# A fused attention, expert and MLP kernel: its float64 weight tiles decoded in another order, their remainders on VectorE

## The chip, the cores and the metric

The kernel runs on one core of a Trainium2 chip. The time is the device time of one execution in microseconds (us), the median of several. The five engines are TensorE (PE, with its weight loads shown apart as PEld), VectorE (DVE), ScalarE (ACT), GpSimd (POOL) and SyncE (SP, which here only issues DMAs). Each engine takes its instructions strictly in the order in which they stand in its own queue; an instruction that waits holds up all that stand behind it on that engine.

## The reference, cut to what matters

Three parts follow one another. A linear attention over (2, 8, 768, 48) gives 1536 token rows of 384. A mixture of 8 experts (width 1024) treats each row with the expert that its gate picks. A gated MLP of width 1536 ends it; its gate weights are drawn 200 times larger than usual.

```python
def _moe2_ref(x, w_gate, w_val, w_out) -> np.ndarray:
    gate = 1.0 / (1.0 + np.exp(-(x @ w_gate)))
    val = x @ w_val
    return (gate * val @ w_out).astype(np.float32)
```

The weights of the MLP arrive as float64. The kernel reads each as two 32-bit words and makes a float32 of it.

## The kernel before, in words

**Precision.** Every float32 product is made of three fp32r matmuls: an operand a is split into a high part (ACT casts it to fp32r) and a low part, the remainder (a less its high part, rounded to fp32r); high by high, high by low and low by high are summed in PSUM.

**The expert stage** (97.7 to 244 us of the trace) runs a loop over 64 steps, eight slices f of eight experts e. Step i holds `s1` (nine matmuls of 256 columns into `ph`, then `hh` on ACT at L825 and its remainder `hl` on DVE at L826), `s2` of three steps before, at two places of each expert the transposes and the split of the next expert's tokens (`etr`: `xh` or `xeh` on ACT at L807, `xl` or `xel` on DVE at L808), and `bg`, which splits one weight tile of 128x768: `rh` on ACT at L137, `rl` at L139, in odd steps on POOL and in even ones on DVE.

**The MLP stage** (from 244 us) takes the 1536 tokens in four blocks j of 384 and the width in twelve slices f. `mf(j,f)` is 18 matmuls of 384 columns into two PSUM tiles `pg`, nine for the gate and nine for the value. `gate` follows: sigmoid `sg` on ACT (L934), product `gg` on DVE (L936), its fp32r cast `gh` on ACT (L939) and its remainder `gl` on DVE (L940). `mo(j,f)` is nine matmuls that add the slice to the output in `po`. The two `pg` tiles have one buffer each: the next `mf` may write its gate half only once `sg` has read the one before, and its value half only once `gg` has. (The first `mf` of blocks 0 and 1 borrows tiles of `po` and waits for neither.) Two lanes run through the loop at L967: lane 0 does block 0 and then 2, lane 1, two steps later, block 1 and then 3. So the order on PE is `mf(0,0)`, `mf(0,1)`, `mo(0,0)`, `mf(0,2)`, `mo(0,1)`, `mf(1,0)`, and from there on one `mf` and one `mo` in turn, 27 matmuls to a gate, lanes alternating.

**The decoding.** A tile of 128x768 float64 weights is fetched by SP into `r64` (two buffers) and decoded in seven steps that `decode` (L151) returns as closures: o1 the magnitude from the upper word into `wf`, on ACT (L157); o2 a clamp (L160), o3 a shift (L163), o4 the sign (L167) and o5 the three bits from the lower word (L171), all on DVE; o6 the fp32r cast of the tile on ACT (L177) and its remainder, the tile less its cast, on POOL (L178); o7 the fetch of the tile two places later in `ORDER` (L149). `wf` has two buffers as well. Tiles 0 to 11 feed `mf`, tiles 12 to 17 feed `mo`. The first seven (`EARLY`) of `ORDER` are decoded in the expert stage, one closure a step from step 6 on (L900), into buffers named `ws`. The other eleven are decoded in the MLP loop, one tile to each k: o1 to o3 ahead of the gate of lane 0, o4 and o5 ahead of that of lane 1, o6 and o7 behind it; they go into the buffers `rh`, `rl` and `raw` (named `wr`) that the expert stage has left.

Nothing reorders any of this: the order of the calls is the order of each queue.

Of the kernel before, what the change touches and what calls it, by code (L numbers as in the profile page):

```python
# [7 lines left out]
F32 = mybir.dt.float32  # L8
# [25 lines left out]
WARM = 16  # L34
BG = (0, 0, 0, 0, 0, 0, 4, 3)
DP = 2
ORDER = (0, 1, 2, 12, 3, 4, 13, 5, 6, 14, 7, 8, 15, 9, 10, 16, 11, 17)
EARLY = 7
HPB = 6
OVP = 60  # L40
# [62 lines left out]
def body(tc, A, out):  # L103
    nc = tc.nc
    E = mybir.EngineType
    with ExitStack() as top, tc.manual_schedule():
# [37 lines left out]
        r64, wyh, wyl = {}, {}, {}  # L144
        spl, homes = [None], []

        def dfetch(n):
            r64[n] = spl[0].tile([128, 768, 2], I32, tag="r64", name="r64", bufs=2)
            nc.sync.dma_start(out=r64[n].rearrange("p a b -> p (a b)"), in_=wy[n])  # L149

        def decode(n):  # L151
            t = {}

            def o1():
                t["a"] = spl[0].tile([128, 768], F32, tag="wf", name="wf", bufs=2)
                t["i"] = t["a"].bitcast(I32)
                nc.scalar.activation(out=t["a"], in_=r64[n][:, :, 1].bitcast(F32), func=AF.Abs, scale=2.0 ** 16)  # L157

            def o2():
                nc.vector.tensor_scalar(out=t["a"], in0=t["a"], scalar1=2.0, scalar2=DMAX, op0=ALU.max, op1=ALU.min)  # L160

            def o3():
                nc.vector.tensor_scalar(out=t["i"], in0=t["i"], scalar1=4, scalar2=1, op0=ALU.logical_shift_left,  # L163
                                        op1=ALU.logical_shift_right)

            def o4():
                nc.vector.scalar_tensor_tensor(out=t["i"], in0=r64[n][:, :, 1], scalar=-2 ** 31, in1=t["i"],  # L167
                                               op0=ALU.bitwise_and, op1=ALU.bitwise_or)

            def o5():  # L170
                nc.vector.scalar_tensor_tensor(out=t["i"], in0=r64[n][:, :, 0], scalar=29, in1=t["i"],  # L171
                                               op0=ALU.logical_shift_right, op1=ALU.bitwise_or)
                r64.pop(n)

            def o6():
                wyh[n], wyl[n] = homes.pop(0)
                nc.scalar.copy(out=wyh[n], in_=t["a"])  # L177
                nc.gpsimd.tensor_sub(wyl[n], t["a"], wyh[n].bitcast(F32))  # L178

            def o7():  # L180
                k = ORDER.index(n)
                if k + 2 < 18:
                    dfetch(ORDER[k + 2])

            return [o1, o2, o3, o4, o5, o6, o7]

        scx, sci = [], []

# [505 lines left out]
        with ExitStack() as ctx:  # L694
# [98 lines left out]
            def eload(e, eng=nc.sync):  # L793
                xr[e] = mp.tile([128, 2, 384], F32, tag="xr", name="xr")
                after(eng.dma_start(out=xr[e], in_=xs_d[e * 1536:e * 1536 + 256, :].rearrange("(b p) d -> p b d", p=128)), scx)
# [52 lines left out]
                nc.vector.tensor_sub(XL[m][:, d], ys[e][m], XH[m][:, d].bitcast(F32))  # L848

            xt[0] = (xeh, xel)  # L850
            dops = [op for n in ORDER[:EARLY] for op in decode(n)]
            dops.reverse()
            fetch(sum(BG) + FIRST)
            eload(1)
            dfetch(ORDER[0])
            dfetch(ORDER[1])
            seq = [(e, f) for e in range(8) for f in range(8)]
# [47 lines left out]
        with ExitStack() as ctx:  # L905
# [9 lines left out]
            def mf(j, f):  # L915
                wh, wl = wyh[f], wyl[f]
                if f == 0 and j < 2 or f == 11 and j == 3:
                    pg = [pop.tile([128, 384], F32, tag="po0" if f else "po1", name="pg") for _ in range(2)]
                else:
                    pg = [pgp.tile([128, 384], F32, tag=f"pg{g}", name="pg") for g in range(2)]  # L920
                seq = [(g, kt) for g in range(2) for kt in range(3)]
                if j == f == 0:
                    seq = [(g, kt) for kt in (0, 2, 1) for g in range(2)]
                c = slice(j * 384, j * 384 + 384)
                last = 1 if j == f == 0 else 2
                for g, kt in seq:
                    w = slice((g * 3 + kt) * 128, (g * 3 + kt) * 128 + 128)
                    for n, (a, b) in enumerate(((wh, XH), (wl, XH), (wh, XL))):
                        nc.tensor.matmul(pg[g], a[:, w], b[kt][:, c], start=(kt == n == 0), stop=(kt == last and n == 2))  # L929
                return pg  # L930

            def gate(j, f, pg):
                sg = qp.tile([128, 384], F32, tag="sg", name="sg")
                nc.scalar.activation(out=sg, in_=pg[0], func=AF.Sigmoid)  # L934
                gg = qp.tile([128, 384], F32, tag="gg", name="gg")
                nc.vector.tensor_mul(gg, sg, pg[1])  # L936
                gh = qp.tile([128, 384], F32R, tag="gh", name="gh", bufs=7)
                gl = qp.tile([128, 384], F32R, tag="gl", name="gl", bufs=7)
                nc.scalar.copy(out=gh, in_=gg)  # L939
                nc.vector.tensor_sub(gl, gg, gh.bitcast(F32))  # L940
                gs[(j, f)] = (gh, gl)
# [21 lines left out]
            def lane(first, k):  # L963
                return (first + 2 * (k // 12), k % 12)

            todo = list(ORDER[EARLY:])
            for k in range(24 + SKEW):  # L967
                ops = decode(todo.pop(0)) if todo else []
                for op in ops[:3]:
                    op()  # L970
                if k < 24:
                    gate(*lane(0, k), mf(*lane(0, k)))
                if 0 < k <= 24:
                    mo(*lane(0, k - 1))
                for op in ops[3:5]:
                    op()
                b = k - SKEW
                if b >= 0:
                    gate(*lane(1, b), mf(*lane(1, b)))
                if 0 < b <= 23:  # L980
                    mo(*lane(1, b - 1), (0, 1, 2) if b < 20 else (0, 1) if b < 22 else (0,))
                for op in ops[5:]:
                    op()
            for f, t in ((7, 2), (8, 2), (9, 2), (9, 1), (11, 0), (10, 1), (11, 1), (10, 2), (11, 2)):
                mo(3, f, (t,))

# [16 lines left out]
```

## Time and profile before

| | us |
|---|---|
| median of 3 runs | 483.82 (483.56 to 485.02) |
| the profiled execution, its own time | 483.43 |
| its span, first to last instruction | 481.7 |
| PE busy in the span | 445.0 (92%) |
| DVE busy | 291.4 (60%) |
| ACT busy | 223.0 (46%) |
| POOL busy | 178.9 (37%) |

The profiled execution's own time is 1.7 us more than its span. PE is busy nearly throughout, so that what matters is where it is not, and who it waits for there; an engine with a low share of busy time can still be the one that is waited for.

### The profile page before, as it was taken

Reading aid. Unit: us, or ns where it says so; the run is one execution under the profiler, and the core shown is the slowest. Engines: PE = TensorE matmul, PEld = TensorE weight load, DVE = VectorE, ACT = ScalarE, POOL = GpSimd, SP = SyncE. Lnnn points to the kernel's source line nnn. Section 1 sums busy time; section 2 is a strip of 40 time slices with the busy share of each in tenths; the row PEclk is TensorE's granted clock in tenths of the full one; section 3 lists DMA queues with packets and bytes.
Section 4 is the critical chain, followed back from the end, with each engine's and each line's share of the span. In section 5 each row is a group of like instructions: output and inputs, shape, how many; then the busy total and the mean of one; then the engine's idle time right before and its main releaser. Section 6 shows DMA issues by size and latency. Waiting matters only on the chain.

```text
span 481.7 us, 8681 instructions
## 1 busy us (share of the span) xinstructions
PE 445.0 (92%) x3354; PEld 429.0 (89%) x3356; DVE 291.4 (60%) x506; ACT 223.0 (46%) x481; POOL 178.9 (37%) x126
## 2 busy tenths in 40 slices
PE   6979987599998999899989899999999999999995
PEld 2668986599988999898988799999999999999995
DVE  4897997678999899987347676566322222212221
ACT  2676877546845775675333433433232322222231
POOL 4786938635866555565002221121120200000022
PEclk9979999799999999999999999999999999999999
DMA  7999942779899777862003322320010100000011
GB/s 212 350 336 309 283 186 84 250 294 208 226 210 353 257 243 243 259 231 71 3 9 123 116 83 67 126 71 0 1 49 1 49 1 0 1 1 1 1 49 49
DMA packets 23708, 65.11 MB, mean 135 GB/s; under 512 B 4592, under 2 KB 8816, under 8 KB 23664
## 3 DMA queue, kind: packets, MB, share of 16 engines
q1 hardware_dynamic: 21600, 59.80, 40.1%
q0 software_dynamic: 1920, 4.73, 2.6%
q8 instruction: 27, 0.44, 0.4%
q14 instruction: 17, 0.14, 0.1%
q10 hardware_dynamic: 144, 0.00, 0.0%
HBM read 56.65 MB, written 7.87 MB: 134 GB/s over the span
## 4 chain that ended last, share of the span: by engine, by line
PE 44%; DVE 3%; issue 3%; ACT 1%; POOL 1%; POOLq 0%; ACTq 0%; DVEq 0%
PE pg L929 28%; PE po L953 5%; PE po L952 5%; PE po L951 4%; DVE wf L160 1%; PE ph L822 1%; DVE gg L936 1%; POOL out_dram L190 1%; DVE wf L167 1%; ACT wf L157 1%; PE py L841 1%; PE py L843 0%; PE py L842 0%; DVE wf L171 0%; DVE gl L940 0%
## 5 line engine op out<-in xcount | busy, mean ns | idle before, releaser
L936 DVE TENSOR_TENSOR gg<-sg,pg 128x384 f32<-128x384 f32 x48 | 26.6, 553 | 93.7 <-PE pg L929 91.7
L929 PE MATMUL pg<-xhi,ws 128*128 128x384 f32 x240 | 61.6, 337 | 4.7 <-ACT sg L934 3.0
L939 ACT CAST gh<-gg 128x384 fp32r<-128x384 f32 x48 | 24.7, 514 | 83.9 <-DVE gg L936 83.9
L139 POOL TENSOR_TENSOR rl<-raw,rh 128x768 fp32r<-128x768 f32 x25 | 49.3, 1975 | 26.6 <-ACT rh L137 24.9
L190 POOL DMA_INDIRECT out_dram<-ob,ids x12 | 11.7, 975 | 123.8 <-ACT ob L960 121.4
L934 ACT ACTIVATE sg<-pg 128x384 f32<-128x384 f32 x48 | 23.5, 490 | 70.6 <-PE pg L929 70.6
L137 ACT CAST rh<-raw 128x768 fp32r<-128x768 f32 x64 | 53.2, 839 | 4.3 <-PE py L842 4.2
L841 PE MATMUL py<-hh,rh 128*128 128x256 f32 x192 | 54.2, 282 | 0.0
L842 PE MATMUL py<-hl,rh 128*128 128x256 f32 x192 | 53.1, 276 | 0.0
L843 PE MATMUL py<-hh,rl 128*128 128x256 f32 x192 | 53.1, 276 | 0.0
L929 PE MATMUL pg<-xlo,rh 128*128 128x384 f32 x144 | 48.7, 338 | 0.0
L929 PE MATMUL pg<-xhi,rh 128*128 128x384 f32 x144 | 48.6, 338 | 0.0
L929 PE MATMUL pg<-xhi,rl 128*128 128x384 f32 x144 | 48.6, 337 | 0.0
L929 PEld LDWEIGHTS pg<-xhi,ws 128*128 128x128 f32 x240 | 43.1, 188 | 6.2 <-ACT sg L934 3.6
L139 DVE TENSOR_TENSOR rl<-raw,rh 128x768 fp32r<-128x768 f32 x32 | 42.3, 1321 | 6.1 <-ACT rh L137 5.6
L940 DVE TENSOR_TENSOR gl<-gg,gh 128x384 fp32r<-128x384 f32 x48 | 26.8, 558 | 27.8 <-ACT gh L939 27.8
L178 POOL TENSOR_TENSOR rl<-wf,rh 128x768 fp32r<-128x768 f32 x8 | 14.7, 1837 | 70.5 <-ACT rh L177 70.5
L929 PE MATMUL pg<-xlo,ws 128*128 128x384 f32 x120 | 40.2, 335 | 0.0
L841 PEld LDWEIGHTS py<-hh,rh 128*128 128x128 f32 x192 | 36.1, 188 | 0.1
L825 ACT ACTIVATE hh<-ph 128x256 fp32r<-128x256 f32 x64 | 24.8, 388 | 24.6 <-PE ph L822 23.6
L842 PEld LDWEIGHTS py<-hl,rh 128*128 128x128 f32 x192 | 36.1, 188 | 0.0
L843 PEld LDWEIGHTS py<-hh,rl 128*128 128x128 f32 x192 | 36.0, 188 | 0.0
(187 smaller groups left out, 1230.7 us busy)
## 6 DMA issues: line engine op xcount, KB each, us to landing
raw<-in_wx_dram SPq DMA_DIRECT2D x64, 384.0 KB, 5.4
r<-in_wy_dram SPq DMA_DIRECT2D x18, 768.0 KB, 4.4
dm<-in_dm_dram SPq DMA_DIRECT2D x8, 672.0 KB, 11.6
kr<-in_kr_dram SPq DMA_DIRECT2D x8, 576.0 KB, 11.7
v<-in_v_dram SPq DMA_DIRECT2D x8, 384.0 KB, 10.7
xs_d<-zero SPq DMA_DIRECT2D x8, 384.0 KB, 10.6
xr<-xs_d SPq DMA_DIRECT2D x8, 384.0 KB, 4.3
cat<-in_cax_dram SPq DMA_DIRECT2D x1, 404.0 KB, 13.6
```

The lines of the kernel that those rows point to most:

```text
L137: nc.scalar.copy(out=h, in_=t)
L139: (nc.gpsimd if pool else nc.vector).tensor_sub(rl[n % NR], t, h.bitcast(F32))
L825: nc.scalar.activation(out=hh, in_=ph, func=AF.Relu)
L841: nc.tensor.matmul(y, wh[:, w], hh, start=(f == 0 and m != 1), stop=False, skip_group_check=True)
L842: nc.tensor.matmul(y, wh[:, w], hl, start=False, stop=False, skip_group_check=True)
L843: nc.tensor.matmul(y, wl[:, w], hh, start=False, stop=(f == 7), skip_group_check=True)
L929: nc.tensor.matmul(pg[g], a[:, w], b[kt][:, c], start=(kt == n == 0), stop=(kt == last and n == 2))
L936: nc.vector.tensor_mul(gg, sg, pg[1])
L939: nc.scalar.copy(out=gh, in_=gg)
L940: nc.vector.tensor_sub(gl, gg, gh.bitcast(F32))
L952: nc.tensor.matmul(po[j][t], gh[:, a], wl[:, w], start=False, stop=False)
L953: nc.tensor.matmul(po[j][t], gl[:, a], wh[:, w], start=False, stop=(f == 11))
```

## The change

`decode` hands back eight closures in place of seven: the remainder becomes o8 and goes from POOL to DVE. `ORDER` is changed so that a tile for `mo` comes one place earlier.

In the expert stage the seven early tiles keep one closure a step, but the fetch (o7) comes ahead of the cast (o6), and the last of the seven steps now does the cast and the remainder together.

In the MLP stage the eleven tiles are taken in pairs (n, m), three groups of closures to a pair: o1 of n, the two remainders (o8) of the pair before, o2 and o3 of n; then o4, o5, fetch and cast of n, o1 and o2 of m; then o3, o4, o5, fetch and cast of m. One group stands behind each gate, of lane 0 and of lane 1 alike, beginning behind the first gate; before, a tile's steps began ahead of the gate of lane 0.

```diff
-ORDER = (0, 1, 2, 12, 3, 4, 13, 5, 6, 14, 7, 8, 15, 9, 10, 16, 11, 17)
+ORDER = (0, 1, 2, 12, 3, 4, 13, 5, 14, 6, 7, 15, 8, 9, 16, 10, 11, 17)
...
                 nc.scalar.copy(out=wyh[n], in_=t["a"])
-                nc.gpsimd.tensor_sub(wyl[n], t["a"], wyh[n].bitcast(F32))
+
+            def o8():
+                nc.vector.tensor_sub(wyl[n], t["a"], wyh[n].bitcast(F32))
...
-            return [o1, o2, o3, o4, o5, o6, o7]
+            return [o1, o2, o3, o4, o5, o6, o7, o8]
...
-            dops = [op for n in ORDER[:EARLY] for op in decode(n)]
+            dops = []
+            for n in ORDER[:EARLY]:
+                d = decode(n)
+                dops += [d[0], d[1], d[2], d[3], d[4], d[6], lambda d=d: (d[5](), d[7]())]
...
-            todo = list(ORDER[EARLY:])
+            def groups():
+                work = [decode(n) for n in ORDER[EARLY:]]
+                last = []
+                for i in range(0, len(work), 2):
+                    n = work[i]
+                    m = work[i + 1] if i + 1 < len(work) else None
+                    yield [n[0]] + last + [n[1], n[2]]
+                    yield [n[3], n[4], n[6], n[5]] + ([m[0], m[1]] if m else [n[7]])
+                    if m:
+                        yield [m[2], m[3], m[4], m[6], m[5]]
+                        last = [n[7], m[7]]
+                yield last if len(work) % 2 == 0 else []
+
+            todo = list(groups())
+
+            def some():
+                for op in todo.pop(0) if todo else []:
+                    op()
+
             for k in range(24 + SKEW):
-                ops = decode(todo.pop(0)) if todo else []
-                for op in ops[:3]:
-                    op()
                 if k < 24:
                     gate(*lane(0, k), mf(*lane(0, k)))
                 if 0 < k <= 24:
                     mo(*lane(0, k - 1))
-                for op in ops[3:5]:
-                    op()
+                if k < 24:
+                    some()
                 b = k - SKEW
                 if b >= 0:
                     gate(*lane(1, b), mf(*lane(1, b)))
+                    some()
...
-                for op in ops[5:]:
-                    op()
```

**ACT at the start of the MLP stage, before.** `wf_3549` is tile 5, `wf_3587` tile 6; `sg` and `gh` are of the gates (0,0), (0,1) and (0,2) in turn.

```order
L157 ACTIVATE wf_3549<-r64_2895 128x768
L934 ACTIVATE sg_3573<-pg_3553 128x384
L939 CAST gh_3577<-gg_3575 128x384
L177 CAST rh0_68<-wf_3549 128x768
L157 ACTIVATE wf_3587<-r64_3114 128x768
L934 ACTIVATE sg_3611<-pg_3591 128x384
L939 CAST gh_3615<-gg_3613 128x384
L177 CAST rh1_69<-wf_3587 128x768
L157 ACTIVATE wf_3637<-r64_3585 128x768
L934 ACTIVATE sg_3661<-pg_3641 128x384
```

Behind every gate stand the cast of one tile and o1 of the next, ahead of the next sigmoid.

**ACT at the same place, after.** `wf_3577` is tile 5, `wf_3626` tile 14, `wf_3700` tile 6, `wf_3748` tile 7 (the lines of the gate are five further on than before); `sg` of (0,0), (0,1), (0,2), (1,0), (0,3).

```order
L939 ACTIVATE sg_3569<-pg_3549 128x384
L944 CAST gh_3573<-gg_3571 128x384
L157 ACTIVATE wf_3577<-r64_2866 128x768
L939 ACTIVATE sg_3601<-pg_3581 128x384
L944 CAST gh_3605<-gg_3603 128x384
L177 CAST rh0_68<-wf_3577 128x768
L157 ACTIVATE wf_3626<-r64_3081 128x768
L939 ACTIVATE sg_3649<-pg_3629 128x384
L944 CAST gh_3653<-gg_3651 128x384
L177 CAST rh1_69<-wf_3626 128x768
L939 ACTIVATE sg_3692<-pg_3672 128x384
L944 CAST gh_3696<-gg_3694 128x384
```

The first sigmoid now stands in front of all decoding; from there on o1, cast and o1, and cast stand between the sigmoids in a turn of three gates.

**DVE over two gates of both lanes, before** (tile 7 in `wf_3712`).

```order
L160 TENSOR_SCALAR wf_3712<-wf_3712 128x768
L163 TENSOR_SCALAR wf_3712<-wf_3712 128x768
L936 TENSOR_TENSOR gg_3738<-sg_3736,pg_3717 128x384
L940 TENSOR_TENSOR gl_3741<-gg_3738,gh_3740 128x384
L167 SCALAR_TENSOR_TENSOR wf_3712<-r64_3635,wf_3712 128x768
L171 SCALAR_TENSOR_TENSOR wf_3712<-r64_3635,wf_3712 128x768
L936 TENSOR_TENSOR gg_3777<-sg_3775,pg_3756 128x384
L940 TENSOR_TENSOR gl_3780<-gg_3777,gh_3779 128x384
```

**DVE over three gates, after** (tiles 6 and 7 in `wf_3700` and `wf_3748`; L180 is the remainder).

```order
L160 TENSOR_SCALAR wf_3700<-wf_3700 128x768
L163 TENSOR_SCALAR wf_3700<-wf_3700 128x768
L941 TENSOR_TENSOR gg_3728<-sg_3726,pg_3707 128x384
L945 TENSOR_TENSOR gl_3731<-gg_3728,gh_3730 128x384
L167 SCALAR_TENSOR_TENSOR wf_3700<-r64_3623,wf_3700 128x768
L171 SCALAR_TENSOR_TENSOR wf_3700<-r64_3623,wf_3700 128x768
L160 TENSOR_SCALAR wf_3748<-wf_3748 128x768
L941 TENSOR_TENSOR gg_3773<-sg_3771,pg_3752 128x384
L945 TENSOR_TENSOR gl_3776<-gg_3773,gh_3775 128x384
L163 TENSOR_SCALAR wf_3748<-wf_3748 128x768
L167 SCALAR_TENSOR_TENSOR wf_3748<-r64_3669,wf_3748 128x768
L171 SCALAR_TENSOR_TENSOR wf_3748<-r64_3669,wf_3748 128x768
```

Before, every second gate has no decoding of its own in front of it; now each of the three has some, and behind the third gate of each turn (not shown) come the two remainders.

**ACT in the expert stage, at the last early tile** (`ws12_1320`), before and then after: the cast stands one step later, behind the next `hh` and the next expert's `xh`.

```order
L825 ACTIVATE hh_3066<-ph_3056 128x256
L137 CAST rh2_70<-raw_2862 128x768
L177 CAST ws12_1320<-wf_2924 128x768
L825 ACTIVATE hh_3093<-ph_3083 128x256
L807 CAST xh_3006<-xp_3097 128x3x128
L137 CAST rh3_71<-raw_2891 128x768
```

```order
L827 ACTIVATE hh_3066<-ph_3056 128x256
L137 CAST rh2_70<-raw_2862 128x768
L827 ACTIVATE hh_3093<-ph_3083 128x256
L809 CAST xh_3006<-xp_3097 128x3x128
L137 CAST rh3_71<-raw_2891 128x768
L177 CAST ws12_1320<-wf_2924 128x768
```

The cast moved past one `hh` and one `xh`; its remainder, before on POOL, now follows on DVE.

## Rows read from the trace of the kernel before

**Rows 1.** Busy us by stretch: length, PE, PEld, DVE, ACT, POOL; clock, DMA, GB/s.

```profile
244.40:272.00 27.60, 23.84 (x130) 22.55 (x131) 17.72 (x24) 9.94 (x18) 5.48 (x3) 1.00 0.25 86
272.00:330.00 58.00, 58.00 (x333) 58.00 (x333) 38.62 (x52) 21.25 (x37) 11.08 (x6) 1.00 0.24 82
330.00:464.00 134.00, 134.00 (x767) 134.00 (x766) 35.95 (x62) 33.93 (x68) 9.56 (x8) 1.00 0.03 10
```

**Rows 2.** Waits of PE: who waited for whom, total us, times, longest.

```profile
PE pg L929 <- ACT sg L934: 3.0, 2, 1.9
...
PE ph L822 <- DVE xl L808: 2.7, 3, 1.9
...
PE pg L929 <- DVE gg L936: 0.8, 2, 0.4
```

**Rows 3.** Timeline, tile 5 through the MLP's first gates: start, duration, instruction, idle before.

```profile
244.38 0.62 PE L929 MATMUL pg<-xhi,ws 128*128 128x384 f32 x2 [0.92 <-DVE xlo L848]
...
244.76 0.56 DVE L160 TENSOR_SCALAR wf<-wf 128x768 f32<-128x768 f32 x1 [0.44 <-ACT wf L157]
...
245.35 0.56 DVE L163 TENSOR_SCALAR wf<-wf 128x768 int32<-128x768 int32 x1
...
247.29 0.49 ACT L934 ACTIVATE sg<-pg 128x384 f32<-128x384 f32 x1 [2.63 <-PE pg L929]
...
247.86 0.56 DVE L936 TENSOR_TENSOR gg<-sg,pg 128x384 f32<-128x384 f32 x1 [1.95 <-ACT sg L934]
...
248.45 0.51 ACT L939 CAST gh<-gg 128x384 fp32r<-128x384 f32 x1 [0.67 <-DVE gg L936]
...
249.47 0.95 DVE L167 SCALAR_TENSOR_TENSOR wf<-r,wf 128x768 int32<-128x768 int32 x1
...
251.50 0.84 ACT L177 CAST rh<-wf 128x768 fp32r<-128x768 f32 x1 [2.54 <-DVE wf L171]
...
252.24 0.90 ACT L157 ACTIVATE wf<-r 128x768 f32<-128x768 f32 x1
...
252.42 1.82 POOL L178 TENSOR_TENSOR rl<-wf,rh 128x768 fp32r<-128x768 f32 x1 [22.93 <-ACT rh L177]
253.05 0.47 ACT L934 ACTIVATE sg<-pg 128x384 f32<-128x384 f32 x1
253.17 1.48 DVE L160 TENSOR_SCALAR wf<-wf 128x768 f32<-128x768 f32 x1 [1.76 <-ACT wf L157]
...
253.57 0.61 PE L929 MATMUL pg<-xhi,ws 128*128 128x384 f32 x2 [1.09 <-ACT sg L934]
...
254.69 0.56 DVE L163 TENSOR_SCALAR wf<-wf 128x768 int32<-128x768 int32 x1
...
255.16 0.55 DVE L936 TENSOR_TENSOR gg<-sg,pg 128x384 f32<-128x384 f32 x1
```

**Rows 4.** Timeline: second stall, a later `gg`, start of `mf(0,9)`, its sigmoid.

```profile
268.94 0.61 PE L929 MATMUL pg<-xhi,ws 128*128 128x384 f32 x2 [1.92 <-ACT sg L934]
...
292.02 0.55 DVE L936 TENSOR_TENSOR gg<-sg,pg 128x384 f32<-128x384 f32 x1 [1.13 <-PE pg L929]
...
321.53 0.19 PEld L929 LDWEIGHTS pg<-xhi,rh 128*128 128x128 f32 x1
...
323.54 0.49 ACT L934 ACTIVATE sg<-pg 128x384 f32<-128x384 f32 x1 [0.48 <-PE pg L929]
```

**Rows 5.** Groups by line: the 128x768 remainders on DVE, without and beside POOL's.

```profile
L139 DVE TENSOR_TENSOR rl<-raw,rh 128x768 fp32r<-128x768 f32 x32 | 42.3, 1321 | 6.1 <-ACT rh L137 5.6 <-DMA raw<-in_wx_dram 0.3
...
L640 DVE TENSOR_TENSOR rl<-raw,rh 128x768 fp32r<-128x768 f32 x3 | 2.7, 948 | 0.0
```

**Rows 6.** The early tiles' cast in the expert stage: waits in total, then timeline.

```profile
ACT ws L177 <- DVE wf L171: 13.8, 6, 3.7
...
221.00 0.83 ACT L177 CAST ws<-wf 128x768 fp32r<-128x768 f32 x1 [3.69 <-DVE wf L171]
...
222.54 0.38 PE L822 MATMUL ph<-xh,rh 128*128 128x256 f32 x1 [0.98 <-ACT xh L807]
```

## The prediction

> **What bounds the kernel now.** I read busy time by stretch first. In the MLP from 272 us on PE is busy without a break (58.00 of 58.00 us, then 134.00 of 134.00), while DVE is at two thirds and ACT at a third [rows 1]. So the MLP runs at PE's pace, and a change there can only add time behind 272 us; what can be won lies before it, where PE is busy 23.84 of 27.60 us. PE's pace is 134.00/767 = 0.1747 us a matmul [rows 1]: 4.72 us for a gate of 27, 14.15 for three.
>
> Next the waits of PE. In the MLP it waited twice for `sg` and twice for `gg`, 3.8 us together [rows 2], all before 272 us; in the expert stage mainly for the split of the next expert's tokens (`xl`, [rows 2]).
>
> Then the timeline of the first stall [rows 3]. The gate half of `mf(0,2)` may start when `sg(0,1)` has read the `pg` before. That sigmoid began only at 253.05, because two steps of decoding stood in front of it on ACT: the cast of tile 5, which had itself waited 2.54 us for o5 on DVE, and o1 of tile 6. PE started at 253.57 after 1.09 us idle. The second stall, at 268.94, is of the same kind [rows 4].
>
> What the reader should take from these rows is a loop: ACT and DVE hand the decoding and the gates to one another, each queue in order, so that nearly every instruction waits for the last one of the other engine. Its length, not either engine's busy time, decides whether PE waits.
>
> **The change part by part: the loop in the MLP.** I go by steps from start to start, which contain the hand-over [rows 3]: o1 to o2 0.93 (252.24 to 253.17); o2 to o3, which depends on it, 0.59 (244.76 to 245.35); a clamp or shift to a `gg` queued behind it 0.47 (254.69 to 255.16); `gg` through `gh` and `gl` to the next DVE step 1.61 (247.86 to 249.47); o4 through o5 to the cast 2.03 (249.47 to 251.50); cast to the next ACT step 0.74; o1 to a sigmoid 0.81 (252.24 to 253.05); `sg` to `gg` 0.57 (247.29 to 247.86); start of `sg` to PE 0.52 (253.05 to 253.57).
>
> Before, one tile is decoded in two gates: o1, o2, o3, `gg`, o4, o5, the second `gg`, its `gh`, cast, next o1. With o2 to o3 at 1.52 (253.17 to 254.69, POOL's remainder running beside it) that makes 0.93 + 1.52 + 0.47 + 1.61, then o4, o5 and `gg` to the cast about 2.9, and 0.74: some 8.2 us for two gates of 9.43. It fits, and the rows say so: at 292.02 it is `gg` that waits 1.13 us for PE [rows 4]. Only where a tile had one gate (the first k) did PE wait.
>
> After, POOL is idle in this stage, so o2 costs 0.59. The remainder costs 0.948 alone on DVE (its three rows without POOL, [rows 5]), +0.03 to a waiter. o1 of the first tile of a pair needs a `wf` buffer, and that is free only when the remainder of the pair before has read it. This closes the loop for a pair and three gates: remainder to o1 0.98, to o2 0.93, to o3 0.59, to `gg` 0.47, to o4 1.61, to the cast 2.03, to o1 of the second tile 0.74, to its o2 0.93, to `gg` 0.47, to o3 1.61, to o4 0.59, to the cast 2.03, to `sg` 0.74, to `gg` 0.57, to the next pair's remainder 1.61. Sum **15.90 us, where PE needs 14.15**. So each pair should hold PE up by 1.75 us, shared by two stalls of some 0.9, until the pairs run out.
>
> Where this begins: I start from `gg(0,0)` and `gh` at 247.86 and 248.45 [rows 3], whose places the change leaves alone. `gh` occupies ACT 0.42 (its 0.51 less the 0.1 by which starts overlap), so o1 of tile 5 is at 248.87, o2 249.80, o3 250.39. `gg(0,1)` waits for PE: 36 matmuls from 244.38 plus 0.1 for the restart and 0.44 to the reader (323.54 less nine matmuls from 321.53, [rows 4]), 251.2. From there o4 252.8, cast 254.8, o1 of tile 14 255.6, its o2 256.5, `gg(0,2)` 257.0, o3 258.6, cast 261.2, `sg(1,0)` 261.95, its `gg` 262.5, the remainder of tile 5 264.1, o1 of tile 6 265.1, `sg(0,3)` 265.9, and PE may start `mf(1,1)` at 266.4. PE gets there after 117 matmuls, at 264.9. That is a first stall of 1.5 us where the kernel before had by then two. Then four pairs, (6,7), (15,8), (9,16), (10,11): the last one's remainder-to-start point is 264.1 + 3 x 15.9 = 311.8, its third `sg` comes 13.72 later at 325.5, and PE starts `mf(0,9)` at 326.0. In the trace that start is 321.53 [rows 4]. Tile 17 alone has a shorter loop (no second tile) and should cost under 0.2. **MLP: +4.5 us**, with bounds of +2.4 (each of the 15 steps 0.03 shorter, over the 4.7 turns up to there) and +5.5 (remainders at 1.2 us). Weights come in time: tile 15, the tightest, is done about 297 and read by `mo(0,6)` after 305.
>
> **Fetches.** `ORDER` and the earlier o7 move SP's fetches ahead, by a step in the expert stage, where raw tiles queue behind; before, DVE's waits for raw tiles there come to 0.3 us in all [rows 5], so I cost it at nothing, up to +0.5 if that reserve is gone.
>
> **The expert stage.** Two things help. The cast of an early tile waited on ACT for o5, 13.8 us in six waits [rows 6], with `hh` and `xh` queued behind; it now comes a step (some 2 us) later, when o5 is done. At the last tile that wait was 3.69 us, and PE's stall of 0.98 on `xh` at 222.54 follows directly behind it [rows 6]. And POOL loses seven remainders that held up DVE. One thing hurts: seven remainders come to DVE, 0.95 alone and 1.32 on the mean of those beside POOL [rows 5], 6.6 to 9.2 us on an engine whose own remainders of this kind already take 42.3 us there, two of them shortly before an expert changes. I take -1.5: the stall at 222.54 goes with its tail, part of one more. The bounds are -3.5 (all stalls that stand shortly behind a cast go) and +3 (DVE becomes the bound and a third of the 9.2 us shows).
>
> Sum: 483.43 (profiled) + 4.5 - 1.5 = 486.4; the runs' median lies 0.4 above the profiled time, and with half of that I say **486.6** (0.2 is added to the rivals' times as well).
>
> **A rule that is weighed.** o2 took 0.56 at 244.76, with POOL idle, and 1.48 at 253.17, while POOL's remainder ran from 252.42 to 254.24 [rows 3]. The Trainium skill (SBUF — State Buffer, Who interferes with whom) has GpSimd share a port pair with VectorE, and the one that comes second blocks fully; the row agrees. By that rule alone DVE pays 0.95 for its remainder and wins 0.93 back on o2, and the MLP would cost nothing. A second rule speaks against my forecast: the skill (Perfetto Trace Analysis, Identifying the Most-Contended Engine) takes occupancy as a fair measure for VectorE, and by it an engine at two thirds has room; that is the first rival.
>
> **Rivals.** *The loop fits (faster).* If the 15 steps come to 14.15 or less, 0.12 less each, PE never waits behind the first pair. Then the MLP has one stall of about 1.5 in place of the four of 3.8 [rows 2], -2.3, and with -1.5 the time is 479.8. For it: DVE's 38.62 of 58.00 [rows 1]. Against: each step is measured, and the same steps give 253.05 and 253.57 before to the hundredth.
>
> *DVE becomes the bound of the expert stage (slower still).* +4.5 + 3 gives 491.1. For it: 1.32 a remainder [rows 5]; against: the long waits of ACT that go [rows 6].
>
> *The two cancel.* A loop of 15.5 (+2.6 or so) and an expert stage at -2.5: about 483.7. For it: 13.8 us of ACT waits [rows 6]; against: little of these reached PE.
>
> *The change does not do what it says:* were `wf` free without the remainder, o1 could run early; but then the two remainders stand ahead of o2 on DVE (0.88 each), and `gg` to o2 takes 3.37 in place of 3.52. The loop shrinks by 0.15 only; it belongs to the forecast.
>
> **How the numbers follow.** Forecast 0.66, cancelled 0.14, DVE-bound 0.12, loop fits 0.08. A difference of about 0.3%, 1.45 us, is what a measurement of this kernel can tell from none. Slower by more: 0.60 of the forecast's 0.66 and the DVE-bound case, 0.72; within: 0.06 and the cancelled case, 0.20; faster: 0.08. The range, from the cancelled case to the bounds of the forecast on the far side (+5.5, +0.5): 483.6 to 489.8; it leaves out the loop that fits (0.08) and most of the DVE-bound case (0.10 of 0.12).
>
> **What would show it.** In the changed trace: `pg` waiting for `sg` again and again until about 326 us, in turns of 15.9 us, 8 to 9 us in total; o2 at 0.55 throughout the MLP; no wait of the `ws` cast for o5; `mf(0,9)` about 3 us later than 321.5. No PE gaps behind 270 us, or none that recur, would prove the loop wrong; gaps in front of the experts that grow would prove the -1.5 wrong.

## The result, and the profile after

The changed kernel takes 488.16 us (median of 20 executions, 483.09 to 491.3), the kernel before 484.32 on the same chip (20, 482.55 to 487.49). Two executions, the one at 491.3 and one of recut_three_gates at 483.93, lie over 1.5% above the fastest of their kernel and stay out of the ratios. The ratio is 1.0064, with a 95% interval of 1.0046 to 1.0082: slower by 3.1 us (the medians lie 3.8 apart), where 486.6 was forecast and "slower by over 0.3%" had a chance of 0.72. The profiled execution took 487.12 us, its span 485.3.

The MLP by stretch, columns as in [rows 1]:

```profile
244.16:272.00 27.84, 25.65 (x144) 25.01 (x144) 16.03 (x25) 10.48 (x18) 0.00 (x0) 1.00 0.20 65
272.00:330.00 58.00, 53.77 (x296) 51.53 (x297) 40.10 (x60) 22.01 (x37) 0.00 (x0) 1.00 0.26 92
330.00:464.00 134.00, 134.00 (x768) 133.89 (x767) 34.98 (x62) 31.81 (x65) 5.87 (x6) 1.00 0.03 10
```

PE, busy 58.00 of 58.00 us between 272 and 330 before, is now busy 53.77, though no engine is near its limit: DVE has 40.10, ACT 22.01, POOL nothing. Ahead of 272 PE has become better, behind 330 it is full again.

PE's waits in the MLP (who for whom, us in total, times, longest), then ACT's for o5 and for remainders there, then ACT's for the early tiles' cast in the expert stage:

```profile
PE pg L934 <- ACT sg L939: 6.4, 9, 1.4
```

```profile
ACT rh L177 <- DVE wf L171: 22.5, 8, 3.1
ACT wr L177 <- DVE wf L171: 8.1, 3, 3.1
ACT wf L157 <- DVE rl L180: 6.2, 4, 1.5
ACT wf L157 <- DVE wr L180: 1.5, 1, 1.5
```

```profile
ACT ws L177 <- DVE wf L171: 0.2, 1, 0.2
```

Every cast of the MLP now waits for o5, some 2.8 us each (30.6 in eleven); before, that was the case at the first tiles alone. The early tiles' cast waits 0.2 us in place of 13.8 [rows 6].

One stall of PE in the expert stage has grown, the one on `xl` at a change of experts, from 0.54 us before (first line) to 2.76 after (second):

```profile
185.82 0.38 PE L822 MATMUL ph<-xl,rh 128*128 128x256 f32 x1 [0.54 <-DVE xl L808]
```

```profile
188.28 0.39 PE L824 MATMUL ph<-xl,rh 128*128 128x256 f32 x1 [2.76 <-DVE xl L810]
```

The prediction named gaps in front of the experts that grow as what would prove the -1.5 wrong, so in this execution that sign is there.

The starts of the last seven of the nine stalls on PE, in order of time (start, duration, instruction, idle before):

```profile
277.85 0.62 PE L934 MATMUL pg<-xhi,ws 128*128 128x384 f32 x2 [0.52 <-ACT sg L939]
...
288.18 0.62 PE L934 MATMUL pg<-xhi,ws 128*128 128x384 f32 x2 [0.60 <-ACT sg L939]
...
293.72 0.44 PE L934 MATMUL pg<-xhi,rh 128*128 128x384 f32 x1 [0.55 <-ACT sg L939]
...
304.05 0.44 PE L934 MATMUL pg<-xhi,rh 128*128 128x384 f32 x1 [0.62 <-ACT sg L939]
...
309.58 0.44 PE L934 MATMUL pg<-xhi,rh 128*128 128x384 f32 x1 [0.53 <-ACT sg L939]
...
319.86 0.44 PE L934 MATMUL pg<-xhi,rh 128*128 128x384 f32 x1 [0.55 <-ACT sg L939]
...
325.38 0.44 PE L934 MATMUL pg<-xhi,rh 128*128 128x384 f32 x1 [0.53 <-ACT sg L939]
```

Two stalls a turn, and every second start is 15.87, 15.86 and 15.80 us (277.85 to 325.38) behind the one before, where PE's own work would take 14.15. The whole stage, from the first `pg` matmul to the last instruction, is 485.30 - 244.16 = 241.14 us; before, 481.70 - 244.38 = 237.32. This length repeats to a few hundredths between kernels that share the stage, as long as the granted clock in it is the same, so one profile measures it; that of the expert stage does not, and there the times decide.

### The profile page after: what moved, and what is told of

Same layout as the page of the kernel before. It is cut to its first block, busy times and chain, and to the rows that moved or that the text cites. A ratio compares the mean times of both kernels' runs of the same rounds, so it can differ in the third digit from the quotient of the medians.

```text
span 485.3 us, 8678 instructions
## 1 busy us (share of the span) xinstructions
PE 446.8 (92%) x3354; PEld 429.2 (88%) x3356; DVE 294.9 (61%) x524; ACT 224.6 (46%) x481; POOL 143.8 (30%) x108
## 4 chain that ended last, share of the span: by engine, by line
PE 33%; DVE 9%; issue 5%; ACT 4%; POOL 1%; POOLq 0%; ACTq 0%; DVEq 0%
PE pg L934 21%; PE po L958 3%; PE po L956 3%; PE po L957 3%; DVE wf L171 2%; DVE wf L167 2%; ACT wf L157 2%; DVE gg L941 2%; ACT gh L944 2%; DVE gl L945 1%; PE ph L824 1%; DVE wf L163 1%; DVE rl L180 1%; DVE wf L160 1%; ACT sg L939 1%
## 5 line engine op out<-in xcount | busy, mean ns | idle before, releaser
L139 DVE TENSOR_TENSOR rl<-raw,rh 128x768 fp32r<-128x768 f32 x32 | 41.1, 1285 | 5.8 <-ACT rh L137 5.7
L934 PE MATMUL pg<-xhi,rh 128*128 128x384 f32 x120 | 41.1, 342 | 2.8 <-ACT sg L939 2.8
L934 PE MATMUL pg<-xlo,rh 128*128 128x384 f32 x120 | 40.5, 338 | 0.0
L934 PE MATMUL pg<-xhi,rl 128*128 128x384 f32 x120 | 40.5, 337 | 0.0
L329 ACT ACTIVATE at<-cst,dl 128x128 f32<-128x128 f32 x96 | 28.9, 388 | 10.4 <-DVE dl L321 10.3
## 6 DMA issues: line engine op xcount, KB each, us to landing
v<-in_v_dram SPq DMA_DIRECT2D x8, 384.0 KB, 10.8
cat<-in_cax_dram SPq DMA_DIRECT2D x1, 404.0 KB, 13.8
```

Of the source, the lines that this page charges most:

```text
L139: (nc.gpsimd if pool else nc.vector).tensor_sub(rl[n % NR], t, h.bitcast(F32))
L329: nc.scalar.mul(AT[s][:, j, :], ident, dl[:, j:j + 1])
```

## The experiments

Lengths of "the stage" are those of the MLP, taken as above. "Early tiles" are the seven of the expert stage. Ratios are to the kernel before, measured beside it. The 8.3 us of stalls that the expectations give the changed kernel (1.7 a turn, 15.87 - 14.15) count how much later PE starts; the idle time listed above is 6.4.

### Each half alone

**mlp_alone** keeps the changed MLP; the early tiles go back to POOL and the old order:

```diff
-                dops += [d[0], d[1], d[2], d[3], d[4], d[6], lambda d=d: (d[5](), d[7]())]
+                dops += [d[0], d[1], d[2], d[3], d[4], lambda d=d: (d[5](), d[7](nc.gpsimd)), d[6]]
```

> The MLP stage is that of the changed kernel; the seven early tiles are decoded as in the kernel before (cast, then POOL's remainder, then the fetch). The loop theory: all of the loss comes from the MLP stage, in turns of 15.87 us, so mf(0,9) starts 81.2 us after the MLP's first matmul (77.15 before) and the time is 484.3 + 4.1 = 488.4 us. Its repeats lie as close together as those of the kernel before (about 1 us around their middle), if the wide scatter of the changed kernel (483.1 to 491.3) belongs to the expert stage. The rival, that part of the loss is paid in the expert stage: 486 us, and the scatter stays.

Measured: 489.98 against 486.22, ratio 1.0074 (1.0047 to 1.0102), +3.6 us; six repeats between 489.45 and 490.68. The stage is 241.13 us, 3.8 longer than before. So the MLP accounts for the whole loss. Its repeats lie within 1.2 us, where the changed kernel spreads over 8.2, so the changed MLP is not where that scatter comes from.

**early_alone** is the other half: `ORDER` and the MLP of before, the early tiles as changed.

> Only the seven early tiles are decoded as in the changed kernel (fetch ahead of the cast, the cast a step later, remainder on DVE); ORDER and the MLP stage are those of the kernel before. The prediction's term: 484.3 - 1.5 = 482.8 us. The one profile of the changed kernel, in which the MLP began 0.2 us earlier: 484.1. The rival, that DVE becomes the bound of the expert stage: 484.3 + 3 = 487.3. The long wait of ACT for o5 is gone in each case. If the scatter of the changed kernel comes from POOL and DVE holding each other up here, the repeats of this kernel spread over 4 us or more.

Measured: 484.49, ratio 0.9964 (0.9939 to 0.9990), -1.7 us, stage 237.34; the -1.5 of the prediction lies in the interval. The repeats run from 481.18 to 486.21, but those of the kernel before beside it cover almost as much (483.70 to 488.30), so this run does not show that the early tiles' change adds scatter. The halves add up to +1.9 us, the whole is +3.1; the intervals of the halves, 1.3 us to either side each, allow that.

### Which part of the early tiles' change wins

**late_cast_pool** changes the order alone, **dve_old_order** the engine alone:

```diff
-                dops += [d[0], d[1], d[2], d[3], d[4], d[6], lambda d=d: (d[5](), d[7]())]
+                dops += [d[0], d[1], d[2], d[3], d[4], d[6], lambda d=d: (d[5](), d[7](nc.gpsimd))]
```

```diff
-                dops += [d[0], d[1], d[2], d[3], d[4], d[6], lambda d=d: (d[5](), d[7]())]
+                dops += [d[0], d[1], d[2], d[3], d[4], lambda d=d: (d[5](), d[7]()), d[6]]
```

> As early_alone (which came out at 0.9964 of the kernel before, 1.7 us faster), but the early tiles' remainders stay on POOL: only the order is changed, fetch ahead of the cast and the cast a step later. The theory of the prediction: the gain comes from the cast that no longer stands in ACT's queue waiting for o5 (13.8 us of waits), and the remainder on DVE is a small loss or nothing: 1.7 to 2.5 us faster than before, 0.995 to 0.9965. The rival, that the gain comes from POOL being relieved: no gain here, 1.000. The MLP stage is that of the kernel before, 237.3 us from its first matmul to the last instruction.

> The other half alone: the early tiles' remainders on DVE, the order of the kernel before (cast right behind o5, fetch last). The prediction's theory: the cast waits on ACT as before and nothing is won, between 0 and +1 us, 1.000 to 1.002. The rival, POOL relieved: the gain of early_alone is here, -1.7 us or more, 0.9964 or less. The MLP stage is that of the kernel before, 237.3 us.

Measured: late_cast_pool 485.43 against 484.83, ratio 1.0014 (0.9989 to 1.0039), and dve_old_order 486.43, ratio 1.0057 (1.0032 to 1.0083). The order alone wins nothing that can be measured, outside the 0.995 to 0.9965 that my reason gave; the engine alone costs 2.8 us, more than the 0 to 1 expected. The stages are 237.31 and 238.16 us; in the second, TensorE's granted clock was 0.98 over the first 86 us of the stage (1.00 in all the others). In late_cast_pool ACT's wait for o5 is nearly gone, and nothing is won by it, since PE now stalls longest at another place (first ACT's waits, then PE's timeline):

```profile
ACT ws L177 <- DVE wf L171: 1.0, 2, 0.7
```

```profile
170.72 0.39 PE L824 MATMUL ph<-xel,rh 128*128 128x256 f32 x1 [2.15 <-DVE xel L810]
```

So my reason for the -1.5, the 13.8 us of ACT's waits, falls, and so does the rival, POOL's relief. What PE waits for is `xl` and `xel`, and how late these are depends on more than either half. Why the two changes together win 1.7 us where neither wins alone stays open (early_alone ran on another chip, beside its own repeats of the kernel before).

### Is it the loop, DVE's load, or the wait for a buffer?

**old_loop_dve**: loop, `ORDER` and early tiles of before, the late remainders on DVE behind their casts.

> The MLP loop and ORDER of the kernel before, early tiles as before; only the remainders of the eleven late tiles go to DVE, right behind their casts. The loop theory: o2 is no longer held up by POOL (0.56 in place of 1.48) and the remainder of 0.95 runs while ACT does the next o1 (0.9), so the loop of two gates shrinks from 8.2 to 7.4 us and the loss of the changed kernel is in its grouping, not in the move to DVE: PE's stalls in the MLP, 3.8 us before, fall to 1.4 to 1.8, and the stage from 237.3 to 235.0 to 235.4 us. The rival, that the remainder on DVE is what costs: 237.3 or more, up to 241.

Measured: stage 481.20 - 246.34 = 234.86, a little under what was expected and 2.5 us shorter than before. None of PE's waits is for `gg`, and for `sg` there are (us in total, times, longest):

```profile
PE pg L934 <- ACT sg L939: 1.9, 2, 1.1
```

In the old loop the move to DVE is a gain; it loses only together with the new grouping.

**loop_pool**: the changed grouping, the remainders on POOL:

```diff
-                    yield [n[0]] + last + [n[1], n[2]]
+                    yield [n[0], n[1], n[2]]
...
-                        yield [m[2], m[3], m[4], m[6], m[5]]
+                        yield [m[2], m[3], m[4], m[6], lambda m=m: (m[5](), m[7](nc.gpsimd))]
```

> The changed kernel's grouping of the MLP loop (pairs in three gates), with the remainders of the late tiles on POOL right behind their casts, as before. By steps: o1 of the next pair no longer waits behind two remainders, which takes 1.6 us out of the turn of 15.87, but o2 is again held up by POOL (1.48 for 0.56), once or twice in a turn and other steps of DVE with it. The loop theory: the turn stays over PE's 14.15, between 15.2 and 16.0 us, PE's stalls between 5 and 9.5 us, the MLP stage between 239 and 242 us (237.3 before, 241.1 in the changed kernel). The rival, that the remainders on DVE are what costs in the MLP: without them the stage is back at 237.3 or less.

Measured: stage 481.30 - 240.34 = 240.96, with one longer stall a turn, 15.73, 15.72 and 15.68 us apart (274.32, 290.05, 305.77, 321.45 us). Without a single remainder on DVE the loss is the same to 0.2 us. One turn on DVE, a `gg` and the o2 of the second tile:

```profile
293.59 0.56 DVE L941 TENSOR_TENSOR gg<-sg,pg 128x384 f32<-128x384 f32 x1 [0.46 <-PE pg L934]
...
298.84 1.57 DVE L160 TENSOR_SCALAR wf<-wf 128x768 f32<-128x768 f32 x1 [1.70 <-ACT wf L157]
```

The two remainders took 1.6 us of the turn (from `gg` to o2 3.59 us in the changed kernel, 1.95 here). Of this 1.0 is lost again on the second o2, beside POOL's remainder (1.57 in place of 0.56), and about half a us on a `gg` that now waits for PE. So the rival is excluded, but in this grouping POOL and DVE only exchange one delay for another; the recut kernels below decide.

**four_buffers**: `wf` gets four buffers in place of two.

> The changed kernel with four buffers for wf in place of two (room is made by six buffers for gh and gl in place of seven and two for ob in place of three), so that o1 never waits for a remainder. The prediction said that this link matters little, since the two remainders stand ahead of o2 on DVE anyway: the turn 15.7 us in place of 15.87, PE's stalls up to 330 us 7 to 7.7 us. The rival, that the wait of o1 for the remainder (7.7 us in five waits in the changed kernel) is the cause: the turn falls by 1 us or more, and the stalls to 4 or less. Behind 430 us the fewer buffers of gh and gl may cost something; this is not part of the comparison.

Measured: starts at 281.19, 296.81, 312.43 and 327.98 us, turns of 15.62, 15.62 and 15.55; idle 5.5 us in nine stalls in place of 6.4. `mf(0,9)` starts 80.25 us behind the MLP's first matmul in place of 81.22; the stage as a whole, 241.27, is no shorter, and what loses it again in the last 25 us was not traced. ACT no longer waits for a remainder at all, 7.7 us of waits are gone, and the turn is shorter by 0.25 us (0.15 in the prediction). A wait that a trace names last is not what it costs: behind it stood the next one.

**one_step_less** leaves out one link, o4 of each pair's second tile (so five tiles have no signs):

```diff
-                        yield [m[2], m[3], m[4], m[6], m[5]]
+                        yield [m[2], m[4], m[6], m[5]]
```

> The changed kernel with one instruction of the loop left out: o4 (the sign) of the second tile of each pair, so the weights of five tiles lose their signs. The loop theory: the turn shrinks by exactly that step from start to start, 0.87 to 0.95, from 15.87 to 14.9 to 15.0 us for a pair, PE's stalls to about 0.8 in a turn in place of 1.7 and 4 to 4.5 us in all in place of 8.3; the stage from 241.1 to 237.0 to 237.5 us. The rival, that PE is held up by single waits that have nothing to do with the length of the loop: the turn stays at 15.7 or more, the stage at 240 or more.

Measured, on PE:

```profile
289.68 0.61 PE L934 MATMUL pg<-xhi,ws 128*128 128x384 f32 x2 [0.41 <-ACT sg L939]
...
304.59 0.45 PE L934 MATMUL pg<-xhi,rh 128*128 128x384 f32 x1 [0.45 <-ACT sg L939]
...
319.39 0.44 PE L934 MATMUL pg<-xhi,rh 128*128 128x384 f32 x1 [0.36 <-ACT sg L939]
```

Turns of 14.91 and 14.80 in place of 15.87, stage 236.39, 0.6 below what was expected, with 2.8 us idle in five stalls. A DVE instruction of 0.95 left out shortens the turn by 1.0: the loop is the bound.

**recut_three_gates** has the same instructions on the same engines at the same pace, two tiles to three gates, cut at other places: a tile's o1 to o5 stand together behind one gate, its cast and remainder behind the next.

```diff
...
+                for i in range(len(work)):
+                    n = work[i]
...
+                    yield last[:1] + [n[0]] + last[1:] + [n[1], n[2], n[3], n[4], n[6]]
+                    last = [n[5], n[7]]
+                    if i in (0, 2, 4, 6, 8):
+                        yield []
+                yield last
...
```

> The changed kernel with the loop cut differently and the same instructions on the same engines at the same pace (two tiles to three gates): o1 to o5 and the fetch of a tile stand together behind one gate, its cast and its remainder behind the next that has decoding, so that ACT's cast never stands in the queue ahead of a sigmoid while o5 is still to run. The loop theory: DVE's own row for three gates is 3 x 1.61 + 2 x 3.85 = 12.5 us (0.3 wait for the cast, then 0.87, 0.47, 0.47, 0.87, 0.87 from start to start), under PE's 14.15, so the turn is 14.2 to 14.4, PE's stalls fall from 8.3 to 1 to 3 us, and the time is 488.2 - 6 = about 482. The rival, that the load of DVE or the remainders on it are the cause, whatever the order: the same stalls of about 8 us, 488.

**recut_two_gates** puts an empty group behind tiles 0, 1, 2, 3, 5, 6 and 8.

> As recut_three_gates, but most tiles get two gates (an empty group behind the tiles 0, 1, 2, 3, 5, 6 and 8 of the eleven). The loop theory: no stall of over 0.2 us in the MLP, neither the four of the kernel before (3.8 us) nor the nine of the changed one; mf(0,9) starts 73.4 to 73.9 us after the first matmul of the MLP, and with the expert stage of the changed kernel (-0.2 to -1.5) the time is 479.3 to 480.8 us. The rival, DVE's load as the cause: DVE does the same work over somewhat more time, stalls of 4 us or more remain, 484 or more.

Measured: recut_three_gates has a stage of 233.78 us with one stall of 1.31, 477.48 us (median of three) against 486.22, ratio 0.9839 (0.9790 to 0.9887); recut_two_gates a stage of 232.17, 479.15 us, ratio 0.9860 (0.9825 to 0.9895). The second by stretch:

```profile
242.43:272.00 29.57, 29.57 (x170) 29.57 (x170) 17.82 (x27) 10.59 (x19) 0.00 (x0) 1.00 0.23 81
272.00:330.00 58.00, 58.00 (x333) 57.94 (x333) 43.42 (x64) 23.52 (x40) 0.00 (x0) 1.00 0.24 82
```

DVE is busier than in the changed kernel, 43.42 us of 58 against 40.10, and PE does not wait once behind the stage's first matmul. One turn on ACT and DVE shows why:

```profile
281.09 0.51 ACT L944 CAST gh<-gg 128x384 fp32r<-128x384 f32 x1 [1.69 <-DVE gg L941]
281.51 0.83 ACT L177 CAST rh<-wf 128x768 fp32r<-128x768 f32 x1
282.24 0.91 ACT L157 ACTIVATE wf<-r 128x768 f32<-128x768 f32 x1
283.62 0.49 ACT L939 ACTIVATE sg<-pg 128x384 f32<-128x384 f32 x1 [0.46 <-PE pg L934]
```

```profile
282.37 0.96 DVE L180 TENSOR_TENSOR rl<-wf,rh 128x768 fp32r<-128x768 f32 x1 [0.18 <-ACT rh L177]
283.25 0.55 DVE L160 TENSOR_SCALAR wf<-wf 128x768 f32<-128x768 f32 x1
283.84 0.56 DVE L163 TENSOR_SCALAR wf<-wf 128x768 int32<-128x768 int32 x1
284.43 0.96 DVE L167 SCALAR_TENSOR_TENSOR wf<-r,wf 128x768 int32<-128x768 int32 x1
285.42 0.96 DVE L171 SCALAR_TENSOR_TENSOR wf<-r,wf 128x768 int32<-128x768 int32 x1
286.30 0.55 DVE L941 TENSOR_TENSOR gg<-sg,pg 128x384 f32<-128x384 f32 x1
```

The cast stands behind a `gh` that itself came after o5, so it finds its tile done; the remainder fills the time of the next o1 on DVE; the sigmoid waits for PE. In both recut kernels none of the eleven casts of the MLP waits for o5, where in the changed kernel all do (30.6 us). `ORDER`, engines and instructions are those of the changed kernel, and in recut_three_gates so is the pace; only the grouping differs, and nine stalls become one.

### The stall at 188 us

Seven of the profiled kernels have the early tiles of the changed kernel, and so the same order in the expert stage. They fall into three groups. At the change of experts near 185 us PE stalls for `xl` by 2.75 or 2.76 us in four of them and by about 1 (0.94 to 1.22) in early_alone, recut_two_gates and loop_pool; in three of the four with the long stall TensorE's granted clock has fallen by its end.

What tells the first two apart is one collision. In the changed kernel, on DVE (o3, o4, `xl`) and on POOL:

```profile
182.48 2.20 DVE L163 TENSOR_SCALAR wf<-wf 128x768 int32<-128x768 int32 x1
184.60 0.41 DVE L828 SCALAR_TENSOR_TENSOR hl<-ph,hh 128x256 fp32r<-128x256 f32 x1
184.94 2.49 DVE L167 SCALAR_TENSOR_TENSOR wf<-r,wf 128x768 int32<-128x768 int32 x1
187.35 0.41 DVE L828 SCALAR_TENSOR_TENSOR hl<-ph,hh 128x256 fp32r<-128x256 f32 x1
187.68 0.54 DVE L810 TENSOR_TENSOR xl<-xp,xh 128x384 fp32r<-128x384 f32 x1
```

```profile
184.81 1.81 POOL L139 TENSOR_TENSOR rl<-raw,rh 128x768 fp32r<-128x768 f32 x1 [0.54 <-ACT rh L137]
```

In recut_two_gates:

```profile
185.02 0.94 DVE L167 SCALAR_TENSOR_TENSOR wf<-r,wf 128x768 int32<-128x768 int32 x1
...
186.22 0.55 DVE L810 TENSOR_TENSOR xl<-xp,xh 128x384 fp32r<-128x384 f32 x1
```

```profile
185.05 2.59 POOL L139 TENSOR_TENSOR rl<-raw,rh 128x768 fp32r<-128x768 f32 x1 [0.70 <-ACT rh L137]
```

Whoever comes first runs at its own pace, and the other pays: POOL ahead by 0.13 us, and o4 takes 2.49; DVE ahead by 0.03, and o4 takes 0.94 and POOL 2.59. `xl`, two instructions behind o4, and PE follow. All seven profiles bear this out: in the four with the long stall POOL is ahead by 0.13 or 0.14 us; in early_alone and loop_pool it comes 1.00 and 0.98 us behind o4, which takes 0.94. What makes POOL early or late (it waits for `rh` of ACT here) was not followed further.

The clock, by stretch in four_buffers (PE, PEld, DVE, ACT, POOL, granted clock, DMA, GB/s), where PE stands idle 0.62 and 2.75 us up to 188.90 us:

```profile
184.00:188.00 4.00, 1.53 (x12) 1.16 (x10) 4.00 (x4) 1.10 (x2) 2.71 (x2) 1.00 0.99 369
190.00:194.00 4.00, 4.00 (x21) 4.00 (x21) 1.75 (x4) 1.66 (x3) 0.00 (x0) 0.50 0.62 189
194.00:198.00 4.00, 4.00 (x32) 4.00 (x32) 2.17 (x4) 2.76 (x6) 1.84 (x1) 0.88 0.81 299
```

The first matmul behind the stall takes 0.58 us there, and 0.39 in the changed kernel (the line at 188.28 above):

```profile
188.90 0.58 PE L824 MATMUL ph<-xl,rh 128*128 128x256 f32 x1 [2.75 <-DVE xl L810]
```

0.50 is the lower level, 1.2 GHz. PE does 53 matmuls in these last eight us where the profiled execution of the changed kernel, whose clock stayed at 1.00 behind the same stall, does 73: by estimate 20 x 8.0/73 = 2.2 us are lost. The expert stage starts anywhere from 94.2 to 99.4 us, and an early start (94 to 95 us) brings no early start of the MLP, so I compare the latter: it is at 240.3 to 242.6 us with the short stall, at 244.16 with the long one, and at 247.6 to 248.4 where the clock also falls; with the early tiles as before (three profiles) at 244.4 to 246.6. So, on the mean of three profiles each, the changed expert stage wins 4.0 us with the short stall and loses 2.2 where the clock falls. That the -1.7 is a mean of such cases is likely, but not shown. The repeats of the changed kernel lie likewise in two heaps, five at 483.1 to 485.2 and fifteen at 486.8 to 491.3; that each of these belongs to a group named here was not traced.

**recut_and_skip** takes the collision away: no decoding at every eighth step, the one ahead of the second split.

```diff
-                if T0 <= i and dops:
+                if T0 <= i and dops and (i > 58 or i % 8 != (EB[1]+7)%8):
```

> recut_two_gates (0.986 of the kernel before, about 6.8 us faster), and in the expert stage no closure of the decoding at every eighth step, the one ahead of the step with the second split of the next expert's tokens (xl), so that DVE reaches xl with nothing of the decoding in front of it. The theory: the stalls on xl and xel (0.3 to 2.8 us each) come from a decoding step of DVE held up by POOL shortly ahead of them; they go, and with them the stretch of half clock that follows the long one at about 188 us in some executions: expert stage 143 to 144.5 us from its first ph matmul in place of 146 to 148, time 3 to 4 us under recut_two_gates, 0.978 to 0.981, and repeats that lie closer together. The rival, that the same work on DVE only moves the stalls to other steps: 0.985 to 0.987.

**recut_and_skip_pool** is the same with the early remainders on POOL.

> As recut_and_skip, with the early tiles' remainders on POOL in place of DVE. If the collisions ahead of xl are what counts in the expert stage, where the seven remainders run matters little: within 0.002 of recut_and_skip. If POOL's extra 13 us (7 of 1.84) hold up DVE elsewhere, or DVE's 7 us do, the two differ by 1 us or more.

Measured: 474.47 against 484.77, ratio 0.9778 (0.9741 to 0.9815), and 474.05, ratio 0.9769 (0.9739 to 0.9799). The expert stage is 141.78 and 140.69 us from its first `ph` matmul to the MLP (146.66 before), shorter than the 143 to 144.5 expected; PE's stalls on `xl` and `xel` there are gone, but for one in the first kernel:

```profile
150.05 0.39 PE L824 MATMUL ph<-xl,rh 128*128 128x256 f32 x1 [0.35 <-DVE xl L810]
```

The repeats, 471.62 to 476.85 and 472.99 to 474.28, came closer together only in the second. Whether the seven remainders run on DVE or POOL makes no difference that can be measured. Both kernels beat the one before, by 10.8 and 11.2 us, some 4 of them by the skipped steps (0.9778 against 0.9860 for recut_two_gates). The skip takes away any decoding ahead of `xl`, held up or not; how much of the 4 us is POOL's holding up and how much a decoding step's own 0.9 was not separated.

## Why the prediction was right, and where it was not

**The sum.** The forecast was +4.5 for the MLP and -1.5 for the expert stage, +3.0; measured are +3.1 (2.2 to 4.0). The MLP gave +3.82, so that the changed kernel's own times leave -0.7 (-1.6 to +0.2) for the expert stage, less than early_alone's -1.7; the two intervals overlap from -1.6 to -0.5. That the sum agrees to 0.1 us is luck, since one term was 0.7 too high and the other, by these times, 0.8 too favourable. The upper end of the range, added up like the other sums, is 483.43 + 5.5 + 0.5 + 0.2 = 489.6, not 489.8; nothing hangs on it.

**The loop.** Forecast 15.90 us a turn, measured 15.87. First stall: forecast 1.5 us, 22.0 us behind the MLP's first matmul; measured 1.16 us idle, 21.81 behind it. `mf(0,9)`: forecast 81.6 us behind, measured 81.22. The stage grew by 3.82 us, the term was +4.5. Of the 0.7 missing, 0.17 is the row that I took for before: the one at 321.53 [rows 4] is a weight load, which runs ahead, and the matmul itself started at 321.70; 0.2 lies in the first stall, 0.2 in the turns. The same slip makes the step from PE to a reader 0.44 in the prediction, where the matmul's own start gives 0.27; `gg(0,1)` came 6.6 us behind the MLP's first matmul, not 6.8. A sentence on the change, ahead of the prediction, needs putting right as well: before, too, every `gg` had decoding in front of it on DVE, o2 and o3 or o4 and o5; it was ACT's sigmoids of which every second had none.

**The total of the stalls.** Forecast 8 to 9 us of waits; the trace lists 6.4 in nine, which is under the forecast. As a loss of time the 8 to 9 hold: against recut_two_gates, which has no stall, the changed stage loses 241.14 - 232.17 = 8.97 us, 0.28 more than the idle time for each stall; the stage before lost 5.15 with four stalls of 3.8 us [rows 2], 0.34 more for each. The profile's rows give the reason: idle time is counted from the modelled end of the last matmul, which overlaps the next one when PE runs on (0.34 long, 0.17 apart), and the first matmul behind a stall takes 0.44; 0.17 and 0.10 are 0.27. A kernel without stalls wins more than the waits add up to.

**The port.** o2 takes 0.56 us throughout the MLP, as forecast, and in old_loop_dve the move to DVE gains 2.5 us. The rule of the Trainium skill that was weighed (SBUF — State Buffer, Who interferes with whom) agrees with the rows shown to 0.15 us: o4 takes 2.49 us, and the rest of POOL's instruction and its own 0.94 would be 2.62; POOL, when it is second, takes 2.59, and the rest of o4 and its own 1.81 would be 2.72. By that rule alone the MLP would have cost nothing; the grouping made it cost 3.8.

**Occupancy.** The rule that spoke against the forecast (the Trainium skill, Perfetto Trace Analysis, Identifying the Most-Contended Engine) would have let the loop fit, and it does fit: recut_two_gates runs the same work at 43.42 of 58 us on DVE. DVE had the room; the order did not use it. What occupancy can't tell is whether an in-order queue reaches that share.

**The expert stage.** -1.5 was forecast, early_alone measured -1.7 (-3.0 to -0.5), and the stalls at 204.36 and 222.54 are gone, as forecast for the second. But the reason was wrong. "Two things help", the prediction said: the cast no longer waits on ACT, and POOL is relieved. late_cast_pool has the first alone and wins nothing, dve_old_order has the second, with the remainders on DVE that it brings, and loses 2.8 us. It should have been asked what stands ahead of `xl` on DVE, the instruction that PE waits for [rows 2]; the answer was a decoding step that POOL may hold up by 1.5 us, and at that place the gap grew from 0.54 to 2.76 us. So the size of this term came out near by luck. Nor did the trace of one execution show it: by it alone the MLP began only 0.2 us earlier.

**The rivals.** DVE as the bound of the expert stage, the cancelled case and the loop that fits are excluded by early_alone, mlp_alone and the turn of 15.87. The DVE-bound case was near: in the old order the remainders on DVE do cost 2.8 us (dve_old_order), close to its +3. The case that `wf` is free without the remainder was priced at 0.15 a turn and measured at 0.25.

## What to carry to other kernels

Where two engines hand work to one another in order, add up one round of the loop from start to start, and compare it with the bound engine's own round; neither busy shares nor the waits by name tell it. Place each step so that its input was finished before the instruction ahead of it in its queue: the same work at the same pace then went from nine stalls to one, and at a slightly slower pace to none. In front of the one instruction that the bound engine waits for, leave the queue free of other work, above all of work that another engine can hold up: here that was worth some 4 us.

## What the hardware showed that was not expected

- Which of POOL and DVE comes first by 0.03 or 0.13 us decides over 1.55 us on DVE (0.94 or 2.49), over some 1.7 us of PE's stall, and at times over a further 2.2 us by the clock.
- The same stall of PE (0.6 and 2.75 us idle within 184 to 191 us) was followed by a granted clock of 0.50 in three executions and of 1.00 in a fourth.
- The MLP stage repeated to 0.03 us between kernels that share it (237.32, 237.34, 237.31; 241.14, 241.13), while behind the same expert stage the MLP began anywhere from 240.3 to 248.4 us.
